# Attention and feed-forward in one program: the last tokens of two heads in one padded tile, and a new table of the order

## The chip, the cores and the metric

The kernel runs on one core of a Trainium2 chip. A core has five engines that run beside each other, each in its own order: TensorE (PE, matmuls; its weight loads are listed as PEld), VectorE (DVE), ScalarE (ACT), GpSimd (POOL) and SyncE (SP, which here only issues DMAs). ACT and POOL issue DMAs too. Matmul results land in PSUM, eight banks of which each tile of results takes one; everything else that is computed on lies in SBUF.

The metric is the device time of one execution in microseconds (us). One execution was also taken with the hardware profiler: "span" is the time from its first to its last instruction, and all start times are from the start of that span.

## What is computed

Attention with exponential features over 8 batches, 8 heads, 576 tokens and 64 dimensions, and then a feed-forward layer on all 4608 tokens:

```
def phi(x):
    proj = np.einsum('bhsd,df->bhsf', x, w_phi)
    proj = proj - np.max(np.abs(proj), axis=-1, keepdims=True)
    return np.concatenate([np.exp(proj), np.exp(-proj)], axis=-1)
q_p, k_p = (phi(q), phi(k))
kv = np.einsum('bhsf,bhsd->bhfd', k_p, v)
z = np.sum(k_p, axis=2)
num = np.einsum('bhsf,bhfd->bhsd', q_p, kv)
den = np.einsum('bhsf,bhf->bhs', q_p, z)[..., None] + 1e-06
...
x = np.ascontiguousarray(attn_out.transpose(0, 2, 1, 3)).reshape(B * S, H * D)
h = np.maximum(np.maximum(x @ w1, x @ w2), x @ w3)
return (h @ w_out).astype(np.float32)
```

`w_phi` is 64x128, `w1` to `w3` are 512x768, `w_out` is 768x512; inputs and output are fp32, the matmuls work in bf16.

## The kernel before

**Units.** Attention is done in 16 units of four heads of one batch, so two units make a batch. The four heads are two pairs (`pr`), each with two heads (`ab`). The 576 tokens of a head are 512 main tokens (`SM`), four tiles of 128, and 64 last ones (`ST`), half a tile.

**The steps of a unit**, by the names that the profile shows: q and k are loaded as bf16 by POOL's DMA queue (`qk_bf`), v as fp32 by SP's (`v_raw`), and the last 64 tokens of q in a load of their own (`tail_raw`), which POOL copies into `qk_bf`. The blocks are transposed into `qkT`, by TensorE in the first four units (`tps`), by DMA transposes from SP's queue in the other twelve. TensorE projects them (`psk`, `psq`, and `pst` for the last tokens); DVE takes the largest absolute value of each row (`mk`, `mq`) and ACT the exponentials of k (`Ek`). For q a second projection gives the features on the partitions (`psm`), and ACT makes `Eq` of it. ACT makes `em` from `mk`, POOL multiplies v by it (`vab`), and TensorE sums `kvps` over the tokens, copied to `kv_sb`. Then come the **numerators**: TensorE multiplies `Eq` by `kv_sb` into two PSUM tiles `psn`, one for each sign of the exponent, with the denominator as 65th column; DVE scales the first by `sq` (L641), adds the second (L644) and inverts the denominators (`rden`, L689); POOL divides (`x_sb`, L690). The result is transposed into `xT`, by TensorE (`pxT`) in the first two units, by a DMA transpose in the others.

**Numerators before.** They are made in four groups, one for each head: five tiles of 65 columns, of which four are its main tokens and the fifth its last ones. The tile of last tokens holds those of both heads of a pair, 64 rows each, and each head of the pair multiplies the whole tile; half of its rows belong to the other head and are not used. So a unit has 20 tiles of numerators, 40 matmuls. `xT` gets ten blocks of 128 columns for each unit. Since the last tokens of the two heads of a pair land in different columns there, `last` copies one half into place on POOL (L896), and then the whole to where the last chunk reads it (L897).

**Feed-forward.** It runs in nine chunks of 512 tokens: the main tokens of each batch, and a last chunk with the last tokens of all batches. A chunk is 12 `ups` groups of four matmuls (L748), relu or maximum on ACT and DVE into `hT`, and four `ops` groups (L781 with four matmuls, L786 with six), which ACT and DVE copy to `osb` for the stores. The first `ups` of a chunk needs `xT` of both units of its batch and the difference of two weight matrices that POOL makes at the start (`w_bf`, L844). TensorE also turns `w1` (`pwT`) and multiplies it by `w_out` (`pm`) before the first `ops`.

**Order.** Every operation is a node, and the string `PLAN` lists all of them by number, with engine, buffer slots and a start time; the program is written out in that order. On each engine instructions run strictly in it, and semaphores make them wait for what they need. Where the table leaves TensorE free in its first 30 us, `fill` puts matmuls of a constant tile there (`idler`, L911), whose results nobody reads.

Of the kernel before, what the change touches and what calls it, by code (L numbers as in the profile page):

```python
# [8 lines left out]
FP32 = mybir.dt.float32  # L9
# [8 lines left out]
DM = H * D  # L18
# [7 lines left out]
HU = 4  # L26
# [6 lines left out]
XW = SM + P  # L33
# [4 lines left out]
BY_HALF = 0  # L38
BY_BATCH = 99
# [10 lines left out]
TRAW = 2  # L50
WD_PE = 0
# [41 lines left out]
115D@11.1 127A@11.8 1166G@11.5 15D@11.7 27T4@12.1 14D@12.0 117A@12.1 120A@12.5 121A@13.0 1167G@12.3 1169G@13.0 130D1@12.2 28D@12.5 43T76@12.8
21T4@13.0 261G@13.8 129D@12.7 46D@13.1 47D@13.5 54A0@13.6 113A@13.8 78T0@13.3 22D@13.8 36T56@14.3 118D@14.1 125D@14.7 56G0@14.0 44A@14.3
114A@14.5 79A@15.0 23T4@14.6 39D@15.3 40A@15.3 24D@15.9 42D@16.3 48T23@16.4 55G@15.1 137A1@15.8 139G1@16.2 80A@16.0 45A@16.2 50D@16.9
116A@16.5 185G@17.3 58A@17.0 108T4@16.7 37A@17.2 334S0@11.6 140G@18.0 263T0@17.2 57A@17.7 59G@18.2 60G@19.3 267T7@17.7 68T13@17.9 61G@20.4
38A@17.8 49D@17.5 81A0@18.3 109D@18.1 264D2@18.7 268D@19.3 41A@18.5 72A@18.9 71A@19.4 138G@20.5 141A@19.9 131T25@18.8 142G@21.6 144A@20.1
62T46@19.1 64A0@20.2 69A@20.3 63A@20.8 70A@21.0 134T07@19.7 132D@19.5 190T3@20.1 65T26@20.6 1168G@22.7 133D@20.1 156T54@21.2 135D@20.7 82T01@21.6
67A@21.4 66A@21.6 161T6@21.9 136D@21.3 158A1@21.7 191D3@21.8 85T27@22.1 159A1@22.2 143G@23.4 83D0@22.4 160A@22.7 86D@22.9 333G0@24.5 157A@23.2
84D@23.3 164A1@23.7 265T3@22.6 163A@23.9 87D@23.7 332G@25.2 162A@24.1 145T04@23.4 146A1@24.4 151T21@23.9 147A@24.5 194T5@24.3 266D@24.1 155A@24.7  # L100
152A@25.2 195D@24.7 1180T7@24.4 93T60@24.8 153A@25.6 88D0@24.9 89G0@26.0 1181D0@25.0 1172G@27.6 90T34@25.1 154A@26.1 94D1@25.6 148T57@25.7 149A@26.6
91D@26.0 283T62@26.3 1178T3@26.5 165T15@27.0 285A0@26.7 284A0@27.0 95D@26.4 92D@26.8 1176T0@27.3 150A@27.3 287D0@27.2 96D1@27.5 1179A@27.4 168T47@27.7
97G@29.7 286D0@27.6 335G@30.9 196T26@28.1 98T3@28.5 166D2@28.0 1177A@28.3 169D@28.4 200A1@29.2 198A1@29.7 176T14@28.9 197A@30.1 167D@28.8 170D@29.2
276T50@29.4 177D0@29.6 99D@30.0 277A@30.6 173T71@30.1 178D@30.4 100T3@31.0 171D2@30.8 202D1@30.9 1170G@31.1 174D@31.5 278A@31.1 281A@31.6 199D@31.9
280A@32.1 175D@32.5 172G1@33.2 1186T4@31.4 1184T7@32.7 192T2@34.0 279D@32.9 210T15@34.6 179D0@33.5 403G1@34.4 337S0@38.0 189S3@39.4 101A@32.5 1187A@33.1
180G@35.1 201A@33.6 203T34@34.7 1185A@34.2 282D@33.6 208A@35.1 1171G@36.3 1173G@38.4 205A@35.6 262S0@40.0 214D1@34.9 269T60@34.9 270A@36.1 274A@36.5
181T7@35.2 1182T5@35.5 1183A@37.0 193D@35.2 183T2@36.8 473S1@40.6 182D@35.8 209D@36.2 204A@37.5 1188T7@37.1 272D@36.8 184D@37.4 213D@37.8 206D@38.1
271A@38.0 1189A@38.6 1194T5@38.4 207A@39.0 301T26@39.3 212A@39.5 275D@38.7 1175G@40.5 294A0@39.8 402G@42.6 1174G@43.3 221A1@40.0 224A0@40.2 305A0@40.3
288T37@39.6 304A0@40.8 303A@41.2 211A@41.7 1195D1@39.4 338S@42.2 336S2@43.9 297A1@42.0 1202T4@39.9 273A@42.1 302A@42.6 404G@45.4 289D@40.0 223G@45.7
612S0@45.8 290D@40.6 1200T5@40.7 1196T3@41.6 222G@47.7 1203D@41.2 291T76@42.6 228T41@42.8 229A1@43.2 1201D@41.8 1197D@42.7 230A1@43.7 218T50@43.0 293D@43.3  # L110
1206T2@43.3 238T3@44.2 1192T6@44.3 220D@43.9 232A@44.2 219D@44.5 406S1@47.4 1207D@45.1 239A@44.6 240A@44.9 1193A@45.4 215T40@45.3 306T53@45.5 292D@45.7
231A@45.8 216D@46.2 217D@46.8 1214T2@45.8 1204T6@46.7 1215D@47.4 310A@46.3 1205D@48.0 307A@46.8 309A@47.3 475S1@50.0 1198T7@47.5 241A0@47.7 339T14@48.5
# [12 lines left out]
541G@69.6 1226A3@71.3 395D@71.2 610G@70.3 386D@71.6 397D@72.0 485T64@71.8 490A1@72.2 545S2@67.5 492T03@72.0 496D1@72.4 750G2@71.0 398D@72.7 399D2@73.3
387D@73.5 489A1@72.7 486A@73.2 680G@71.7 1238T5@72.2 493A@73.7 491D0@73.9 435G@72.4 546S@75.8 1242T2@73.1 1219S@77.0 494A@73.9 478T37@74.1 487A@74.2
1239A0@74.7 495D@74.5 484D@74.8 391D0@75.4 1243A@75.2 481D@75.5 616S0@77.6 1254T1@74.4 450T4@75.3 451A@75.6 1240T0@75.4 751S1@80.4 544S0@82.0 400G1@74.5
482A@75.9 488D@76.1 1255D@76.7 483A@76.4 452A@76.9 1252T5@76.2 440T26@77.2 613G@75.7 479A@77.1 1241D@77.3 437T74@77.4 480A@77.6 441A@78.1 443A@78.6
1253D@78.1 615S@82.6 547T10@78.6 1236T3@78.9 503A1@79.0 442A@79.2 444A@79.7 439D1@78.8 1234T5@79.7 553D1@79.1 438D@79.7 550D@80.0 505G0@79.4 1237A@80.2
465T42@80.6 466D1@81.1 549A0@80.7 506G@81.5 462T76@80.9 463D@81.5 467D@81.9 1250T3@81.2 548A0@81.2 1235A@81.7 454T41@82.1 551A@82.2 504G@81.6 552A@82.6  # L130
1227A@83.1 510T75@82.5 514A1@83.7 1246T2@82.8 455D0@82.6 464D@83.0 456D@83.4 511A1@84.2 1223S@84.0 468D1@83.8 512A@84.7 392G@83.7 1251D@83.9 457T40@83.7
458D@84.5 401S@85.0 1232T6@84.0 1233A@85.1 1248T1@84.9 561T34@85.8 513A@85.6 1247D@84.9 554T72@85.9 459D@85.5 565D0@86.1 563A@86.1 469G2@84.9 584T60@86.2
562A@86.4 821G3@86.1 460D2@86.5 461G@86.8 1249D@86.6 1244T5@86.5 587A0@86.7 470S@88.1 614S2@89.6 564D@87.2 588A0@87.1 1260T4@87.3 559A@87.6 556A@88.1
500T13@88.3 1245D@87.5 497T05@88.5 1261T@88.8 585A@88.6 586A@89.1 560D@88.2 557D@88.8 572A0@89.5 1256T6@90.1 502D@89.4 520T3@91.0 555A@89.7 684S1@90.2
# [121 lines left out]
def kernel(  # L256
# [82 lines left out]


    units = [dict() for _ in range(UNITS)]
    tails, loads, qk_bufs = {}, {}, [None]

    def k_rows(src, u, p0, p1):
        h0 = (u % 2) * HU
# [597 lines left out]
```

## Time and profile before

| | us |
|---|---|
| median of three runs (281.70, 282.66, 283.45) | 282.66 |
| the profiled execution | 282.56 |
| its span | 280.8 |
| what lies around the span | 1.76 |
| TensorE's first `ups` starts at | 40.81 |
| TensorE's last matmul ends at | 276.2 |

A row of a group reads: line, engine, operation, what is written from what is read, shape, count, then busy time, mean duration of one in ns, and the idle time of the engine just before. A row of the timeline reads: start, length, engine, line, operation, count, and in brackets the idle time before it with what ended it. A row of the windows gives for one stretch its length and then for each engine the busy time and the number of instructions. Operations that follow each other overlap a little, so the time from the start of one to the start of the next is less than the duration of one; both are used below, and named.

### The profile page before, as it was taken

How to read it: one execution, taken by the hardware profiler on the slowest of the kernel's cores; microseconds unless marked ns; L12 is line 12 of the kernel's file. 1: busy time of each engine (PE TensorE's matmuls, PEld its weight loads, DVE VectorE, ACT ScalarE, POOL GpSimd, SP SyncE). 2: the span in 40 equal slices, each digit the busy share in tenths (PEclk: the TensorE clock that was granted, in tenths of full speed). 3: DMA queues.
4: the chain of work that ended last, by engine and by line, in shares of the span. 5: the costliest groups of instructions: out<-in, count | busy, mean ns of one | idle time of the engine just before them, and what ended most of it. 6: DMA issues, size and time to landing. Idle time of an engine off the chain costs nothing. (4 is left out here: it accounts for less than half of the span.)

```text
span 280.8 us, 8401 instructions
## 1 busy us (share of the span) xinstructions
PE 268.3 (96%) x3409; PEld 150.8 (54%) x3447; DVE 217.3 (77%) x442; ACT 199.1 (71%) x489; POOL 161.5 (58%) x161
## 2 busy tenths in 40 slices
PE   8789899999999999999999999999999999999993
PEld 5457654576655555555555456655546544444441
DVE  2799989999999969889997899898876871157320
ACT  4799999999999787698978879989589200310001
POOL 4879999998949703897336848393495341000000
PEclk9999999999999999999999999999999999999999
DMA  7999999997999999999999997717130224110253
GB/s 136 300 202 208 207 173 310 260 164 132 171 186 249 236 196 281 169 171 144 189 263 204 188 276 125 151 55 170 39 86 3 77 47 121 40 75 0 82 144 112
DMA packets 76214, 44.52 MB, mean 159 GB/s; under 512 B 52688, under 2 KB 67344, under 8 KB 76176
## 3 DMA queue, kind: packets, MB, share of 16 engines
q1 hardware_dynamic: 59536, 29.21, 49.8%
q0 software_dynamic: 14912, 11.77, 28.7%
q10 hardware_dynamic: 1728, 3.02, 3.0%
q8 instruction: 27, 0.44, 0.7%
q14 instruction: 11, 0.09, 0.1%
HBM read 34.64 MB, written 9.44 MB: 157 GB/s over the span
## 5 line engine op out<-in xcount | busy, mean ns | idle before, releaser
L748 PE MATMUL ups<-xT,w_bf 128*128 128x512 bf16 x414 | 101.3, 379 | 1.0
L584 ACT ACTIVATE Eq<-psm 128x512 bf16<-128x512 f32 (+1 forms) x160 | 81.7, 587 | 5.4 <-PE psm L593 3.1
L548 POOL TENSOR_TENSOR vab<-v_raw,em 128x1152 bf16<-128x1152 f32 (+1 forms) x36 | 68.2, 1907 | 22.9 <-ACT em L542 15.0
L504 ACT ACTIVATE Ek<-psk 128x512 bf16<-128x512 f32 x128 | 72.1, 633 | 8.2 <-PE psk L496 6.3
L748 PEld LDWEIGHTS <-w_bf 128*128 128x128 bf16 x432 | 39.2, 98 | 43.9 <-issue 2.3
L690 POOL TENSOR_TENSOR x_sb<-y,rden 128x640 bf16<-128x640 f32 x32 | 39.9, 1256 | 39.5 <-DVE rden L689 39.0
L786 PE MATMUL ops<-wout_bf,hT 128*128 128x512 bf16 (+2 forms) x214 | 50.5, 373 | 0.3
L758 DVE TENSOR_TENSOR hT<-hT,ups 128x512 bf16<-128x512 bf16 x54 | 35.5, 677 | 13.3 <-PE ups L748 11.1
L500 DVE TENSOR_REDUCE mq<-psq 128x4 f32<-128x512 f32 x64 | 41.2, 682 | 3.5 <-PE psq L496 3.2
L500 DVE TENSOR_REDUCE mk<-psk 128x4 f32<-128x512 f32 x64 | 41.9, 679 | 2.1 <-PE psk L496 1.7
L762 ACT ACTIVATE hT<-ups 128x512 bf16<-128x512 f32 x36 | 21.9, 620 | 24.5 <-PE ups L748 24.4
L641 DVE TENSOR_TENSOR y<-psn,sq 128x325 f32<-128x325 f32 x64 | 30.4, 491 | 6.7 <-PE psn L632 4.3
L796 ACT COPY osb<-ops 128x512 f32<-128x512 f32 x20 | 12.2, 608 | 32.3 <-PE ops L786 31.8
L786 PEld LDWEIGHTS <-hT 128*128 128x128 bf16 x222 | 20.6, 98 | 22.5 <-issue 0.2
L632 PEld LDWEIGHTS <-Eq 128*128 128x128 bf16 x640 | 26.3, 98 | 10.3 <-issue 0.4
L644 DVE TENSOR_TENSOR y<-y,psn 128x325 f32<-128x325 f32 x64 | 29.7, 487 | 1.6
L632 PE MATMUL psn<-kv_sb,Eq 128*128 128x65 bf16 x640 | 28.8, 194 | 0.2
L496 PEld LDWEIGHTS <-qkT 64*128 64x128 bf16 x576 | 18.0, 94 | 13.4 <-issue 8.3
L781 PE MATMUL ops<-xT 128*128 128x512 bf16 x87 | 23.7, 380 | 0.5
L567 PE MATMUL kvps<-vab,Ek 64*128 64x65 bf16 x1152 | 22.1, 191 | 0.8 <-POOL vab L548 0.6
L567 PEld LDWEIGHTS <-Ek 64*128 64x128 bf16 x1152 | 20.3, 94 | 3.4 <-issue 1.3
L796 DVE COPY osb<-ops 128x512 f32<-128x512 f32 (+2 forms) x17 | 11.1, 657 | 12.5 <-PE ops L786 12.5
(65 smaller groups left out, 263.9 us busy)
## 6 DMA issues: line engine op xcount, KB each, us to landing
v_raw<-in_v_dram SPq DMA_DIRECT2D x15, 576.0 KB, 6.0
out_dram<-osb SPq DMA_DIRECT2D x23, 256.0 KB, 3.3
qk_bf<-in_k_dram POOLq DMA_DIRECT2D x15, 288.0 KB, 6.9
qk_bf<-in_q_dram POOLq DMA_DIRECT2D x15, 256.0 KB, 8.7
w_bf<-in_moe_w_dram POOLq DMA_DIRECT2D x3, 768.0 KB, 13.2
out_dram<-osb ACTq DMA_DIRECT2D x9, 256.0 KB, 3.4
tail_raw<-in_q_dram SPq DMA_DIRECT2D x16, 64.0 KB, 4.8
wout_bf<-in_moe_w_out_dram POOLq DMA_DIRECT2D x1, 768.0 KB, 19.2
```

The lines of the kernel that those rows point to most:

```text
L500: return nd(kind, {"DVE": 0.598 if n == 4 else 0.331}, lambda: nc.vector.tensor_reduce(dst(m()), ps()[:, 0:n, :], AXX, ALU.max, apply_abso ...
L504: return nd("ek", {"ACT": 0.478 if n == 4 else 0.264}, lambda: nc.scalar.activation(dst(Ek[g]()), ps()[:, 0:n, :], EXP, scale=1.0 - 2.0 * ...
L548: made.append(chosen(n_, lambda n_, g=g, t0=t0, t1=t1: (nc.vector if n_.eng == "DVE" else nc.gpsimd).tensor_tensor(vab()[:, g, t0:t1, 0:D] ...
L567: nc.tensor.matmul(kvps[ab]()[:, pr, g, :], lhsT=Ek[g]()[r, t, :], rhs=vab()[r, g, t, :], start=(pr == prs[0] and g + j == 0), stop=(pr == ...
L584: return nd("eq", {"ACT": 0.478 if n == 4 else 0.264}, lambda: nc.scalar.activation(Eq[g]()[:, t0:t0 + n, :], ps()[:, 0:n, :], EXP, scale= ...
L632: nc.tensor.matmul(psn[g]()[:, i, :], lhsT=Eq[g]()[:, t, :], rhs=kv()[:, pr, ab, g, :], start=True, stop=True)
L641: n_ = nd("xu", {"DVE": 0.064 + 0.0676 * n_t}, lambda: nc.vector.tensor_tensor(yv(y()), ps(0), sq_of(sq()).unsqueeze(len(shape) - 1).to_br ...
L644: return nd("xw", {"DVE": 0.064 + 0.0674 * n_t}, lambda: nc.vector.tensor_tensor(yv(y()), yv(y()), ps(1), ALU.add), [n_], [psn[1], y], loc ...
L690: divs[pr] = nd("x", {"POOL": 1.2}, lambda pr=pr, y=y, rden=rden: nc.gpsimd.tensor_tensor(x_sb()[:, pr].rearrange("p t a d -> p a t d"), y ...
L748: nc.tensor.matmul(ups()[:, o * n:(o + 1) * n], lhsT=w_bf[i + (not plain)][:, ct, jj * P:(jj + 1) * P], rhs=tokens_of(ct)[:, cols] if halv ...
L758: nc.vector.tensor_tensor(dst, dst, src, ALU.max)
L786: nc.tensor.matmul(ops_()[:, 0:hi - lo], lhsT=hT()[:, j, tt * P:(tt + 1) * P], rhs=wout_bf[:, j, lo:hi], start=plain and j == 0, stop=(j = ...
```

## The change

The last tokens are loaded so that heads 0 and 2 share one tile and heads 1 and 3 the other (one load of two DMAs for each unit instead of one for two units). Their exponentials go into a tile of their own, `eq_ends`, that holds for each sign and each tile three pieces of 64 columns: those of the one head, zeros, those of the other. POOL writes the zeros once at the start. A numerator tile of last tokens is then the sum of two matmuls, one with the columns of the first head and zeros, one with zeros and the columns of the second, each with its own head's `kv_sb`. A unit has 16 + 2 = 18 tiles of numerators, taken in three groups of six; the third holds the last tokens. `sq` is made by one activation instead of two. `xT` gets nine blocks for each unit, and `last` is one copy. Options that were switched off are taken out. The table is new.

```
-XW = SM + P
+XB = PT * P
...
-TRAW = 2
+TRAW = 4
...
 PLAN = """
-9G0@1.2 10S0@0.8 3A@1.1 1D@0.8 2G@1.9 16S0@1.3 0G@2.1 103G1@2.7 104G@7.2 4A@1.8 12D@4.0 8G@7.5 6D@4.2 11A@4.0
...
-    xT = const.tile([P, B, CT, XW], BF16, name="xT")
+    xT = const.tile([P, B, 2, XB], BF16, name="xT")
+    eq_ends = const.tile([P, ES, 2, 2, 3, ST], BF16, name="eq_ends")
...
+    n_zero = node("zero", 0, {"DVE": 0.25, "POOL": 0.45}, None, [], [], port=True)
+    chosen(n_zero, lambda n_: (nc.vector if n_.eng == "DVE" else nc.gpsimd).memset(
+        eq_ends.rearrange("p e g r z c -> p (e g r) z c")[:, :, 1, :], 0.0))
...
-        if u % 2 == 0:
-            t_raw = tails["raw"] = buf("tail_raw", TRAW, [P, 2 * HU // 2, D], FP32)
-
-            def load_t(n_):
-                ends = q[b, :, SM:S, :].rearrange("(pr ab) i d -> ab i pr d", ab=2)
-                for ab in range(2):
-                    queue_of[n_.eng].dma_start(t_raw()[ab * D:(ab + 1) * D, :, :], ends[ab])
...
+        t_raw = buf("tail_raw", TRAW, [P, 2, D], FP32)
+
+        def load_t(n_):
+
+            ends = q[b, h0:h0 + HU, SM:S, :].rearrange("(a r) i d -> a i r d", r=2)
+            for a in range(2):
+                queue_of[n_.eng].dma_start(t_raw()[a * ST:(a + 1) * ST], ends[a])
...
-        eqs["t"] = [q_exp(a, psm, 2, g, NQ) for g in range(2)]
...
+        eqs["t"] = [nd("eq", {"ACT": 0.264}, lambda g=g: nc.scalar.activation(
+            Et()[:, g, :, 0:3:2, :], psm()[:, 0:2, :].rearrange("p r (z c) -> p r z c", z=2), EXP, scale=1.0 - 2.0 * g),
+                       [a, n_tab], [psm, Et], locks=[psm]) for g in range(2)]
...
+        sq = buf("sq", MS, [P, UT], FP32)
+        n_sq = nd("S", {"ACT": 0.1}, lambda: nc.scalar.activation(sq(), mq(), EXP, scale=-2.0), reds_q, [mq, sq])
+        x_sb = buf("x_sb", XSB, [P, UT, D], BF16)
+        divs = []
+        for th in range(3):
+            mine = range(6 * th, 6 * th + 6)
+            ends = th == 2
+            prs = range(2) if ends else sorted({t // 8 for t in mine})
+            psn = [bank("psn", [P, 6, W]) for _ in range(2)]
+
+            def nmm(mine=mine, psn=psn):
+                for i, t in enumerate(mine):
+                    for g in range(2):
+                        o = psn[g]()[:, i, :]
+                        if t < NQ:
+                            pr, c, ab = t // 8, t // 2 % 4, t % 2
+                            nc.tensor.matmul(o, lhsT=Eq[g]()[:, 8 * (c % 2) + 4 * pr + 2 * ab + c // 2, :], rhs=kv()[:, pr, ab, g, :],
                                              start=True, stop=True)
...
+                            continue
+                        for pr in range(2):
+                            pad = Et()[:, g, t - NQ, pr:pr + 2, :].rearrange("p z c -> p (z c)")
+                            nc.tensor.matmul(o, lhsT=pad, rhs=kv()[:, pr, t - NQ, g, :], start=(pr == 0), stop=(pr == 1))
...
+            divs.append(nd("x", {"POOL": 0.767}, lambda th=th, y=y, rden=rden: nc.gpsimd.tensor_tensor(
+                x_sb()[:, 6 * th:6 * th + 6, :], y()[:, :, 0:D], rden().to_broadcast([P, 6, D]), ALU.mult),
+                           [n_], [y, rden, x_sb], port=True))
...
+                nc.sync.dma_start_transpose(out=xT[:, b, u % 2, :].rearrange("p (t c) -> p t c", c=P),
+                                            in_=x_sb().rearrange("p t d -> p (t d)"))
...
-        nc.gpsimd.tensor_copy(xT[D:P, b, :, SM:SM + ST], xT[D:P, b, :, SM + ST:XW])
-        nc.gpsimd.tensor_copy(x_last[b // 4][:, :, b % 4 * ST:(b % 4 + 1) * ST], xT[:, b, :, SM:SM + ST])
+        nc.gpsimd.tensor_copy(x_last[b // 4][:, :, b % 4 * ST:(b % 4 + 1) * ST].rearrange("p (u c) n -> p u c n", u=2),
+                              xT[:, b, :, 2 * SM:XB].rearrange("p u (c n) -> p u c n", n=ST))
```

How the instructions stand before and after, at three places. The first is POOL's queue at the program's start, where it loads q and k of the first units (`qk_bf<-in_q_dram`, `qk_bf<-in_k_dram`) and prepares constants; before:

```order
L383 DMA qk_bf<-in_q_dram 128x2x256
L330 MEMSET wph_low 64x128
masks.py:197 MEMSET ident 128x128
masks.py:199 ISA
masks.py:199 AFFINE_SELECT ident<-ident 128x128
L393 DMA qk_bf<-in_k_dram 128x2x576
L430 CAST qk_bf<-tail_raw 128x2x64
L383 DMA qk_bf<-in_q_dram 128x2x256
```

and now:

```order
L332 MEMSET eq_ends 128x8x64
masks.py:197 MEMSET ident 128x128
masks.py:199 ISA
masks.py:199 AFFINE_SELECT ident<-ident 128x128
L373 DMA qk_bf<-in_q_dram 128x2x256
L330 MEMSET wph_low 64x128
L373 DMA qk_bf<-in_q_dram 128x2x256
L378 DMA qk_bf<-in_k_dram 128x2x576
L408 CAST qk_bf<-tail_raw 128x2x64
L378 DMA qk_bf<-in_k_dram 128x2x576
```

The zeros of `eq_ends` and the identity now stand ahead of the first load of q, and the first copy of last tokens behind three loads instead of two.

The second place is SP's queue at the start, which loads k of the first unit (`k_raw`), the last tokens and v; before:

```order
L408 DMA k_raw<-in_k_dram 128x576
L426 DMA tail_raw<-in_q_dram 64x4x64 x4
L408 DMA k_raw<-in_k_dram 128x576
L435 DMA v_raw<-in_v_dram 128x2x576 x2
L426 DMA tail_raw<-in_q_dram 64x4x64 x2
```

and now:

```order
L387 DMA k_raw<-in_k_dram 128x576 x2
L405 DMA tail_raw<-in_q_dram 64x2x64 x6
L413 DMA v_raw<-in_v_dram 128x2x576
L405 DMA tail_raw<-in_q_dram 64x2x64 x4
L454 DMA_TRANSPOSE qkT<-qk_bf 128x8x128
```

Both halves of k of the first unit now come first, the first v stands behind six DMAs of last tokens, and the second v has left this queue (ACT's queue has it).

The third place is DVE at the end of the second unit's numerators, up to the last copy of `xT` that the first chunk waits for (`mk`, `mq` are row maxima of later units, `pm` is the product of `w1` and `w_out`); before:

```order
L641 TENSOR_TENSOR y_894<-psn_901,sq_677 128x325
L500 TENSOR_REDUCE mk_918<-psk_850 128x4
L644 TENSOR_TENSOR y_894<-y_894,psn_903 128x325
L500 TENSOR_REDUCE mk_834<-psk_884 128x4
L689 RECIPROCAL rden_952<-y_894 128x10
L500 TENSOR_REDUCE mk_834<-psk_886 128x4
L500 TENSOR_REDUCE mq_984<-pst_970 128x2
L472 COPY qkT_602<-tps_956 128x1024
L718 COPY xT_75<-pxT_998 128x640
L500 TENSOR_REDUCE mk_918<-psk_976 128x4
L500 TENSOR_REDUCE mk_834<-psk_986 128x4
L718 COPY xT_75<-pxT_1018 128x640
```

and now:

```order
L614 TENSOR_TENSOR y_940<-psn_881,sq_724 128x390
L478 TENSOR_REDUCE mk_493<-pst_917 128x2
L764 CAST xT_75<-pm_925 128x512
L617 TENSOR_TENSOR y_940<-y_940,psn_883 128x390
L478 TENSOR_REDUCE mk_977<-psk_903 128x4
L619 RECIPROCAL rden_986<-y_940 128x6
L478 TENSOR_REDUCE mk_977<-psk_905 128x4
L635 COPY xT_75<-pxT_960 128x384
L635 COPY xT_75<-pxT_982 128x384
L478 TENSOR_REDUCE mk_977<-psk_951 128x4
L478 TENSOR_REDUCE mk_977<-psk_949 128x4
L635 COPY xT_75<-pxT_1017 128x384
```

A product copy (`xT<-pm`) that was ACT's has come to DVE, the last copy of `qkT` there has gone to ACT, and `xT` is filled by copies of three blocks instead of five.

More of the change, by code (lines that the diff above doesn't have):

```diff
@@ L93 @@
[L93 to L100, printed above, removed]
@@ L341 @@
     units = [dict() for _ in range(UNITS)]
-    tails, loads, qk_bufs = {}, {}, [None]
     def k_rows(src, u, p0, p1):
@@ new lines, in attention, with tx @@
+            for th in range(3):
+                pxT = bank("pxT", [P, 3, P], BF16)
+                def tx(th=th, pxT=pxT):
+                    for o in range(3):
+                        t = 6 * th + 2 * o
+                        nc.tensor.transpose(pxT()[:, o, :], x_sb()[:, t:t + 2, :].rearrange("p a d -> p (a d)"), ident)
+                a = nd("X", {"PE": 0.168}, tx, [divs[th], n_ident], [x_sb, pxT])
+                n_ = nd("Xc", {"DVE": 0.265, "ACT": 0.377}, None, [a], [pxT], locks=[pxT])
+                done.append(chosen(n_, lambda n_, th=th, pxT=pxT: copy_on[n_.eng](
+                    xT[:, b, u % 2, 3 * P * th:3 * P * (th + 1)].rearrange("p (a c) -> p a c", c=P), pxT())))
@@ L726, in attention @@
+            done.append(nd("X", {"SP": 1.21}, xdma, divs, [x_sb], xfer=[(72, 18.0, 1.21)]))
         un["done"] = done
@@ new lines, in chunk, with up, ev @@
+        plain = c_i < RAW0
+        for i in range(2 + plain):
+            for j in range(JT):
+                ups = bank("ups", [P, SM])
+                def up(i=i, j=j, ups=ups):
+                    for ct in range(CT):
+                        nc.tensor.matmul(ups(), lhsT=w_bf[i + (not plain)][:, ct, j * P:(j + 1) * P], rhs=tokens_of(ct),
+                                         start=(ct == 0), stop=(ct == CT - 1))
+                a = ff(("up", "up2", "up3")[i], {"PE": 0.863}, up, ready + ([w_nodes[i]] if plain else diffs[i][j // 2]), [ups])
+                if plain:
+                    plains.append((i, j, a))
+                def ev(n_, i=i, j=j, ups=ups):
+                    dst, src = hT()[:, j, :], ups()
+                    if i > 0:
+                        nc.vector.tensor_tensor(dst, dst, src, ALU.max)
+                    elif plain:
+                        copy_on[n_.eng](dst, src)
+                    elif n_.eng == "ACT":
+                        nc.scalar.activation(dst, src, RELU)
+                    else:
+                        nc.vector.tensor_scalar_max(dst, src, 0.0)
+                e = ff(("t1", "h", "h")[i], {"ACT": 0.477, "DVE": 0.598} if i == 0 else {"DVE": 0.598}, None,
+                       [a] + [before.get(j)] * (i > 0), [ups, hT], locks=[ups])
+                before[j] = chosen(e, ev)
+                if i == 1 + plain:
+                    evac.append(e)
```

460 lines of the change are left out of this document (154 added, 306 removed).

## The prediction

> **What bounds the kernel now.** First the page: the span, the engines' shares, TensorE's busy tenths in 40 slices, and the chain that ended last.
>
> ```profile
> span 280.8 us, 8401 instructions
> PE 268.3 (96%) x3409; PEld 150.8 (54%) x3447; DVE 217.3 (77%) x442; ACT 199.1 (71%) x489; POOL 161.5 (58%) x161
> PE   8789899999999999999999999999999999999993
> PE 44%; POOL 1%; issue 0%; ACT 0%; ACTq 0%
> ```
>
> TensorE is busy all along except at both ends, and the chain consists of TensorE alone but for 1% of POOL. A busy share says little about a stage, so next come the windows: per stretch the length, then busy time of PE, PEld, DVE, ACT and POOL. I cut at the events that matter. The second table holds the `idler` matmuls alone, the third their durations.
>
> ```profile
> 0.00:9.30 9.30, 6.57 (x52) 4.16 (x52) 3.45 (x8) 5.16 (x11) 5.49 (x14) 1.00 0.85 191
> 9.30:33.70 24.40, 22.18 (x427) 15.91 (x428) 22.83 (x53) 22.47 (x66) 21.84 (x27) 1.00 1.23 218
> 33.70:40.80 7.10, 7.00 (x63) 4.07 (x66) 6.20 (x15) 6.79 (x14) 7.08 (x6) 1.00 1.17 177
> 40.80:150.00 109.20, 108.02 (x1544) 60.86 (x1562) 100.30 (x206) 98.17 (x243) 78.68 (x71) 1.00 1.17 208
> 150.00:154.00 4.00, 3.36 (x105) 2.26 (x100) 2.60 (x5) 3.23 (x7) 2.84 (x3) 1.00 1.24 217
> 154.00:276.30 122.30, 121.18 (x1235) 63.55 (x1247) 81.90 (x159) 62.69 (x152) 45.52 (x44) 1.00 0.41 99
> 276.30:280.80 4.50, 0.00 (x0) 0.00 (x0) 0.00 (x0) 0.59 (x1) 0.00 (x0) 1.00 0.42 117
> ```
>
> ```profile
> 0.00:9.30 9.30, 5.16 (x26) 1.00 0.85 191
> 9.30:33.70 24.40, 6.29 (x31) 1.00 1.23 218
> ```
>
> ```profile
> L911 PE MATMUL idler<-idle 128*128 128x256 bf16 x14 | 3.2, 415 | 1.1 <-DVE idle L328 1.1
> L911 PE MATMUL idler<-idle 128*128 128x256 bf16 x7 | 1.0, 282 | 0.0
> ```
>
> Up to 33.7 us TensorE does little that counts: 28.75 busy, of which 11.45 are idlers, so 33.7 - 17.3 = 16.4 us are free or filled. There DVE, ACT and POOL are the bound (22.83, 22.47 and 21.84 of 24.4). From 33.7 to 276.3 TensorE idles 0.10 + 1.18 + 0.64 + 1.12 = 3.04 us; this part is its own work. The last 4.5 us are one copy and the last store. The time is thus the start of the first `ups` (40.8), TensorE's work behind it, its few gaps, and a fixed end.
>
> What releases that first `ups` is seen in the timeline: POOL's last division, TensorE's transposes, DVE's copy.
>
> ```profile
> 36.91 1.27 POOL L690 TENSOR_TENSOR x_sb<-y,rden 128x640 bf16<-128x640 f32 x1
> 39.23 0.44 PE L707 MATMUL pxT<-ident,x_sb 128*128 128x128 bf16 x5
> 39.84 0.48 DVE L718 COPY xT<-pxT 128x640 bf16<-128x640 bf16 x1
> 40.81 1.03 PE L748 MATMUL ups<-xT,w_bf 128*128 128x512 bf16 x4
> ```
>
> **The change part by part.** The groups by line, the shapes apart (columns: busy us, mean ns, idle before):
>
> ```profile
> L632 PE MATMUL psn<-kv_sb,Eq 128*128 128x65 bf16 x640 | 28.8, 194 | 0.2
> L641 DVE TENSOR_TENSOR y<-psn,sq 128x325 f32<-128x325 f32 x64 | 30.4, 491 | 6.7 <-PE psn L632 4.3 <-PE psm L600 1.5 <-ACT Eq L584 0.8
> L689 DVE RECIPROCAL rden<-y 128x10 f32<-128x10 f32 x32 | 6.4, 206 | 0.2
> L690 POOL TENSOR_TENSOR x_sb<-y,rden 128x640 bf16<-128x640 f32 x32 | 39.9, 1256 | 39.5 <-DVE rden L689 39.0 <-PE psn L632 0.4
> L548 POOL TENSOR_TENSOR vab<-v_raw,em 128x576 bf16<-128x576 f32 x8 | 9.1, 1154 | 2.5 <-ACT em L542 2.5
> L548 POOL TENSOR_TENSOR vab<-v_raw,em 128x1152 bf16<-128x1152 f32 x28 | 59.1, 2123 | 20.4 <-ACT em L542 12.5 <-issue 6.4 <-DMA v_raw<-in_v_dram 1.6
> L896 POOL COPY xT<-xT 64x256 bf16<-64x256 bf16 x8 | 3.2, 398 | 4.0 <-DMA xT<-x_sb 3.5
> masks.py:197 POOL MEMSET ident<- 128x128 bf16 x1 | 0.2, 224 | 0.0
> L927 POOL MEMSET const-float32-0.0<- 128x1 f32 x1 | 0.1, 98 | 0.2 <-issue 0.2
> 28.56 0.89 DVE L644 TENSOR_TENSOR y<-y,psn 128x325 f32<-128x325 f32 x2
> tail_raw<-in_q_dram SPq DMA_DIRECT2D x16, 64.0 KB, 4.8
> ```
>
> *TensorE.* Two tiles fewer, but each tile of last tokens now takes two matmuls for each sign: 12 + 12 + 8 + 8 = 40 for a unit, as before (640 in 16 units). Nothing is saved. Two transposes fewer in units 0 and 1 are 2 x 0.055 us (five end in 0.44, one lasts 0.22). So the engine that bounds keeps its work. The second group of six spans both head pairs and needs `kvps` of both, but both stand ahead of the numerators in the old order too, so no wait is added.
>
> *DVE.* Two operations of 325 columns start 0.40 apart (0.89 - 0.49). 390 columns are 20% more; between 0.40 (all fixed) and 0.48 (all by column) I take 0.47, as most of it goes with the columns. A unit: 8 x 0.40 = 3.2 becomes 6 x 0.47 = 2.8, and a third reciprocal costs up to 0.21: 0.2 saved a unit, 3 us in all, hidden behind TensorE but for the two units of the ramp (0.4). [...]
>
> *POOL.* The two shapes of `vab` give 969 ns for 576 columns, 1.68 ns each, and 185 ns fixed. A division of 384 is then 0.83, three are 2.49 against 2 x 1.256 = 2.51: nothing. Eight copies of 398 ns go (3.2 us), late and off the path. The zeros: 224 ns for 128 columns and 98 for one make 1 ns a column, so 0.6 us for 512; by the copies of 256 in 398 ns it could be 0.8. With the identity, which also moves ahead, the first load of q starts about 1.1 us later; it is hidden, since `psk` and four exponentials of k now stand before it is needed, and costs up to 1.1 if they run out.
>
> *DMAs.* 16 more loads of last tokens, 0.68 us of SP's time each (2.72 for four), 11 us in all. SP has room, since it waits longer than this, for `osb` alone 33 us:
>
> ```profile
> 1.19 2.72 SPq L426 DMA_DIRECT2D tail_raw<-in_q_dram  x4
> 4.60 0.94 SPq L435 DMA_DIRECT2D v_raw<-in_v_dram  x2
> SPq L800 <- DVE osb L796: 33.0, 9, 14.6
> PE kvps L567 <- POOL vab L548: 0.6, 1, 0.6
> ```
>
> At the start the first v stands behind two k and six of these: 0.74 + 2 x 0.5 + 6 x 0.68 = 5.8 instead of 4.60, 1.2 us later. `vab` waited for `em` then, not for v (below), which hides it; if v comes last, up to 1.2 are lost on POOL.
>
> Transposes of `xT` shrink from ten blocks to nine, off the path. `sq` by one activation saves ACT one of two short ones a unit, hidden.
>
> *The ramp.* Three waits of POOL and DVE show where it is long:
>
> ```profile
> 3.88 0.33 DVE L415 CAST qk_bf<-k_raw 128x320 bf16<-128x320 f32 x1 [2.88 <-DMA k_raw<-in_k_dram]
> 6.06 0.28 POOL L430 CAST qk_bf<-tail_raw 128x128 bf16<-128x128 f32 x1 [2.52 <-DMA tail_raw<-in_q_dram]
> 15.75 3.38 POOL L548 TENSOR_TENSOR vab<-v_raw,em 128x576 bf16<-128x576 f32 x3 [2.53 <-ACT em L542]
> ```
>
> ```profile
> L858 DVE COPY hT<-pwT 128x1024 bf16<-128x1024 bf16 x1 | 0.7, 692 | 0.0
> L500 DVE TENSOR_REDUCE mk<-psk 128x4 f32<-128x512 f32 x64 | 41.9, 679 | 2.1 <-PE psk L496 1.7
> L472 DVE COPY qkT<-tps 128x1024 bf16<-128x1024 bf16 x3 | 2.0, 682 | 0.0
> ```
>
> Ahead of the last copy of `xT` the new order puts on DVE two copies of `w1` turned, one of the product and two maxima more, and two long copies of `qkT` fewer: three long operations, 0.6 each from start to start (0.68 less the 0.09 by which two `y` overlap), 1.8 us. Three short copies of `kv_sb` more and two short operations fewer are about nothing. With the saving of 0.4 it is 1.5 us more work. On POOL it is 0.6 more (the zeros). Against that stands idle time. DVE is idle 5.85 + 1.57 + 0.90 = 8.3 us up to 40.8; the first 3.8 wait for k and stay, 4.5 can be filled: both halves of k now come first, so casts, reductions and last tokens of unit 0 move into 5 to 10 us. POOL's two waits can shrink by what now stands before them. If all 4.5 go, `ups` starts 3.0 us earlier; if nothing, 1.5 later. I take the middle, 0.7 earlier. Behind it TensorE has a little less left: ahead of the first `ups` now stand eight `psq` and two `psm` more, 0.22 us each set at full rate, less the 0.11 of transposes: 0.3 us. For the gaps I take 0.3 off the 3.04, as DVE and POOL carry 3 us less each; bounds are 3.0 off or 3.0 more. Sum, against the profiled run (282.56 = 280.8 + 1.76, 0.1 below the median): 282.56 - 0.7 - 0.3 - 0.3 = 281.26, so 281.2.
>
> **The rivals.**
>
> *Slower: POOL stands for last tokens.* Every cast now waits for two DMAs of its own unit, and `vab` is queued behind it, then `kvps`. Before, a load served two units, and half of the casts found it there. One stand of 2.52 us is in the ramp above; a late `vab` reached TensorE once (0.6). If in two later units POOL stands 2.5 us and TensorE has nothing else in its order, 5.0 are lost: 282.56 - 1.3 + 5.0 = 286.3. It decides from 1.3 us on. Against it: a load lands in 4.8 us and is issued well ahead. Chance 0.09.
>
> *No change.* The ramp's gaps are refilled by its extra work, and what DVE saves is hidden anyway: 282.3. Chance 0.24, as DVE gets 1.5 us more.
>
> *Slower by the clock.* There are 44 idlers for 57. The trace shows 415 ns for each of the first 14 and 282 for the next 7, so TensorE starts slow and rises after some 3.2 us. If it fell again in the ramp, the 15.9 us of real work in 24.4 make 2.1 in 3.2 us, which would double: 283.3. No gap above 1.6 us is seen before. Chance 0.03. [...]
>
> *Much faster.* The ramp's waits nearly all go (2.2 of 3.0), and a third of the gaps: 282.56 - 2.2 - 0.3 - 1.0 = 279.1. For it: POOL's waits and most of DVE's lie before 16 us, where the orders differ most. Chance 0.16.
>
> **How the numbers follow.** The forecast (280 to 282) has 0.48. Below 1% of a difference (2.8 us) this kernel can't be told from no change, so the limits are 279.8 and 285.5: faster 0.18 (the last rival and a little of the forecast), slower 0.07 (most of the first), same 0.75. The range 278.9 to 284.6 leaves out the first rival and half of the last's spread.
>
> **What would show it.** `psn` again 640 matmuls and about 28.8 us; y at 48 + 48 operations near 0.56 us; the first `ups` between 39 and 41 us; idle time of TensorE from there to its last matmul near 2.7; an end of 4.5. It is wrong if the first `ups` starts after 41.5, if `kvps` waits for `vab` by more than 2 us in sum, or if idlers beyond the first 14 last 400 ns.

## The result and the profile after

The changed kernel takes 290.86 us (median of 4, 289.69 to 292.77) against 282.63 before: a ratio of 1.030, 95% interval 1.023 to 1.036. The profiled execution took 290.7 us, of which 288.7 are its span. In e4_x4_early, e5_small_dma, e6_shift and e10_shift_only single executions (two of four, two of ten, three of ten, one of four) took over 1.5% longer than the fastest one; the medians below include them, the ratios leave them out.

First the page of the changed kernel: the span, TensorE's busy time, its tenths in 40 slices, the granted clock in tenths, and the chain that ended last.

```profile
span 288.7 us, 8420 instructions
PE 272.4 (94%) x3432; PEld 150.8 (52%) x3432; DVE 210.6 (73%) x428; ACT 199.2 (69%) x472; POOL 157.3 (54%) x171
PE   8879999999997949999999999999998999999993
PEclk9999999999999996999999999999999999999999
PE 72%; DMA 12%; POOL 7%; ACT 3%; issue 2%; SPq 1%; DVE 1%; POOLq 0%; DVEq 0%; ACTq 0%
```

Two digits of TensorE's row are new, the 7 and the 4, and right behind the 4 the clock has a 6. The chain, TensorE alone before, now runs 12% through DMAs. TensorE's waits name what it stood for (total, times, longest):

```profile
PE ups L660 <- DMA xT<-x_sb: 4.2, 1, 4.2
PE psn L603 <- issue: 1.8, 1, 1.8
PE kvps L546 <- issue: 1.2, 1, 1.2
PE kvps L546 <- POOL vab L527: 0.3, 1, 0.3
```

The timeline gives their places, and the first `ups`; the windows, cut at these places, show TensorE's busy time first and the granted clock behind POOL's.

```profile
39.82 2.76 PE L660 MATMUL ups<-xT,w_bf 128*128 128x512 bf16 x12
88.13 0.22 PE L603 MATMUL psn<-kv_sb,Eq 128*128 128x65 bf16 x2 [1.81 <-issue]
108.67 4.42 PE L660 MATMUL ups<-xT,w_bf 128*128 128x512 bf16 x10 [4.20 <-DMA xT<-x_sb]
213.66 2.43 PE L546 MATMUL kvps<-vab,Ek 64*128 64x65 bf16 x141
```

```profile
85.80:88.10 2.30, 0.52 (x11) 0.39 (x10) 1.14 (x3) 2.07 (x6) 1.72 (x1) 1.00 1.69 277
104.50:108.70 4.20, 0.03 (x1) 0.02 (x1) 1.19 (x4) 2.37 (x6) 1.53 (x2) 0.81 1.28 180
108.70:113.90 5.20, 5.20 (x22) 1.86 (x23) 1.76 (x3) 0.76 (x2) 0.00 (x0) 0.50 1.15 297
215.90:217.40 1.50, 0.25 (x17) 0.13 (x11) 0.19 (x1) 0.12 (x1) 0.00 (x0) 1.00 0.00 0
284.40:288.70 4.30, 0.00 (x0) 0.00 (x0) 0.00 (x0) 0.57 (x1) 0.00 (x0) 0.92 0.38 108
```

So the span's 7.9 us more can be accounted for. The first `ups` starts at 39.8 for 40.8: -1.0. TensorE stands 4.2 for `xT` at 104.5. Behind that the clock is 0.50 for 5.2 us (ten `ups` matmuls take 4.42 us there, twelve took 2.76 at 39.82), and half of it is lost: 2.6. Two stands in the middle of a row of matmuls, put on nothing ("issue"), are 1.8 and 1.25. Less for `vab` (0.6 to 0.3) and a shorter end (4.5 to 4.3) give -0.5. Sum 8.35; the 0.45 over is smaller gaps and work, not taken apart.

Why `xT` was late is on SP's queue and in the DMA issues. First SP's timeline, of before and of the changed kernel, where it transposes `xT` of units 4 and 5:

```profile
90.38 4.11 SPq L722 DMA_TRANSPOSE xT<-x_sb  x2
```

```profile
85.59 1.44 SPq L413 DMA_DIRECT2D v_raw<-in_v_dram  x1
87.20 6.83 SPq L454 DMA_TRANSPOSE qkT<-qk_bf  x2
94.08 0.57 SPq L413 DMA_DIRECT2D v_raw<-in_v_dram  x1
94.69 1.28 SPq L405 DMA_DIRECT2D tail_raw<-in_q_dram  x2
96.08 5.25 SPq L639 DMA_TRANSPOSE xT<-x_sb  x2
102.12 2.73 SPq L413 DMA_DIRECT2D v_raw<-in_v_dram  x2
```

Then the issues from 76 to 104 us (count, KB each, median us to landing), of before and of the changed kernel:

```profile
v_raw<-in_v_dram SPq DMA_DIRECT2D x2, 576.0 KB, 5.4
xT<-x_sb SPq DMA_TRANSPOSE x2, 4.2
```

```profile
v_raw<-in_v_dram SPq DMA_DIRECT2D x5, 576.0 KB, 8.8
xT<-x_sb SPq DMA_TRANSPOSE x2, 8.8
```

Five loads of v stand where two stood, and `xT` lands in 8.8 us for 4.2. Over the whole run the 14 transposes of `xT` land in these times, first before, then now:

```profile
DMA to landing us min/median/max: 3.3/3.6/7.2
DMA to landing us min/median/max: 3.2/3.5/10.8
```

The longest, 10.8, is the one that TensorE stands for: unit 5's goes out at 97.9 and lands at 108.6. Before, it went out at 93.1 and landed 3.5 us later. So 4.8 us of its lateness are SP's, which comes to it later, and 7.3 the transfer's. The table tells which are new ahead of `xT`: the loads at 85.6 and 94.1 are v of units 11 and 10, which it sends out at 80.5 and 87.2 of its own time, though their first uses stand at 142 and 135. Theory A: these bytes (or the issues) make `xT` late. Theory B: SP holds `xT` behind transposes of `qkT` that wait for other engines.

### The profile page after: what moved, and what is told of

It is laid out like the page before. It is cut to its first block, busy times and chain, and to the rows that moved or that the text cites. A ratio compares the mean times of both kernels' runs of the same rounds, so it can differ in the third digit from the quotient of the medians.

```text
span 288.7 us, 8420 instructions
## 1 busy us (share of the span) xinstructions
PE 272.4 (94%) x3432; PEld 150.8 (52%) x3432; DVE 210.6 (73%) x428; ACT 199.2 (69%) x472; POOL 157.3 (54%) x171
## 4 chain that ended last, share of the span: by engine, by line
PE 72%; DMA 12%; POOL 7%; ACT 3%; issue 2%; SPq 1%; DVE 1%; POOLq 0%; DVEq 0%; ACTq 0%
PE ups L660 30%; PE ops L697 14%; PE ops L692 10%; PE kvps L546 5%; PE psn L603 5%; DMA xT<-x_sb 4%; DMA v_raw<-in_v_dram 3%; POOL vab L527 3%; DMA qkT<-qk_bf 3%; PE psk L474 2%; PE psm L572 2%; DMA tail_raw<-in_q_dram 2%; PE psq L474 2%; ACT Ek L482 2%; PE psn L608 1%
## 5 line engine op out<-in xcount | busy, mean ns | idle before, releaser
L660 PE MATMUL ups<-xT,w_bf 128*128 128x512 bf16 x432 | 104.0, 385 | 4.2 <-DMA xT<-x_sb 4.2
L482 ACT ACTIVATE Ek<-psk 128x512 bf16<-128x512 f32 x128 | 73.9, 640 | 6.3 <-PE psk L474 4.0
L563 ACT ACTIVATE Eq<-psm 128x512 bf16<-128x512 f32 x128 | 71.7, 630 | 7.5 <-PE psm L572 6.2
L620 POOL TENSOR_TENSOR x_sb<-y,rden 128x384 bf16<-128x384 f32 x48 | 38.9, 824 | 38.9 <-DVE rden L619 28.6
L673 ACT ACTIVATE hT<-ups 128x512 bf16<-128x512 f32 x40 | 24.9, 634 | 23.6 <-PE ups L660 21.9
L614 DVE TENSOR_TENSOR y<-psn,sq 128x390 f32<-128x390 f32 x48 | 26.3, 556 | 4.4 <-PE psn L603 2.2
L617 DVE TENSOR_TENSOR y<-y,psn 128x390 f32<-128x390 f32 x48 | 26.3, 556 | 2.4 <-DVE y L614 0.5
L603 PEld LDWEIGHTS <-Eq 128*128 128x128 bf16 x512 | 21.9, 98 | 10.4 <-issue 3.1
L603 PE MATMUL psn<-kv_sb,Eq 128*128 128x65 bf16 x512 | 24.1, 194 | 1.9 <-issue 1.8
L675 DVE TENSOR_SCALAR hT<-ups 128x512 bf16<-128x512 f32 x14 | 9.3, 685 | 20.7 <-PE ups L660 20.7
```

The source lines that it names most:

```text
L482: return nd("ek", {"ACT": 0.478 if n == 4 else 0.264}, lambda: nc.scalar.activation(dst(Ek[g]()), ps()[:, 0:n, :], EXP, scale=1.0 - 2.0 * ...
L563: return nd("eq", {"ACT": 0.478 if n == 4 else 0.264}, lambda: nc.scalar.activation(Eq[g]()[:, t0:t0 + n, :], ps()[:, 0:n, :], EXP, scale= ...
L603: nc.tensor.matmul(o, lhsT=Eq[g]()[:, 8 * (c % 2) + 4 * pr + 2 * ab + c // 2, :], rhs=kv()[:, pr, ab, g, :], start=True, stop=True)
L620: divs.append(nd("x", {"POOL": 0.767}, lambda th=th, y=y, rden=rden: nc.gpsimd.tensor_tensor(x_sb()[:, 6 * th:6 * th + 6, :], y()[:, :, 0: ...
L660: nc.tensor.matmul(ups(), lhsT=w_bf[i + (not plain)][:, ct, j * P:(j + 1) * P], rhs=tokens_of(ct), start=(ct == 0), stop=(ct == CT - 1))
```

## The experiments

Each is the changed kernel with the edit shown, unless said otherwise.

**The v loads of units 11 and 10 later** (e1_v_late). The two words of the table:

```diff
-822S2@80.5    753S0@87.2
+822S2@127.5   753S0@118.3
```

> The changed kernel with two numbers of its table altered: the v of units 11 and 10 is loaded by SP after 127.5 and 118.3 in the table's time instead of 80.5 and 87.2 (first used at 142 and 135), so both 576 KB loads leave the stretch ahead of the xT transposes of units 4 and 5. Theory A (these early v loads crowd the DMA engines and SP, so xT lands 4.2 us late and TensorE then runs 6.8 us at half rate, 2.6 lost): the wait of ups for xT at 104 falls below 1 us, the clock stays at 1.00, and the time is 290.9 - 6.8 = 284 (283 to 285.5). Theory B (xT is late because SP holds it behind qkT transposes that wait for POOL and TensorE): both stay, 289 to 291.

285.09 us, ratio to before 1.010 (1.005 to 1.015), span 281.9. In the issues of the same stretch three v loads are left, `xT` lands in 6.3, TensorE waits for it nowhere, and the clock is 1.00 throughout. What is left of TensorE's waits is the two stands without a name:

```profile
v_raw<-in_v_dram SPq DMA_DIRECT2D x3, 576.0 KB, 7.4
xT<-x_sb SPq DMA_TRANSPOSE x2, 6.3
```

```profile
PE psn L603 <- issue: 1.8, 1, 1.8
PE kvps L546 <- issue: 1.2, 1, 1.2
```

The span falls by 6.8, which is 4.2 + 2.6 (the medians fall by 5.8; the profiled execution is the fastest of its four). Theory A holds for this wait; theory B, by which it would have stayed, falls.

**The unit 4 transpose earlier** (e4_x4_early).

```diff
-403S@89.4
+403S@80.4
```

> The changed kernel with the xT transpose of unit 4 at 80.4 in the table instead of 89.4, ahead of a v load, two qkT transposes, another v load and tail loads on SP; unit 5's stays. Theory B (xT held behind the others on SP): the two transposes no longer run one behind the other, unit 5's lands 2 to 4 us sooner, the wait falls to 0.5 to 2 us with no half rate: 284 to 287. Theory A (traffic, and unit 5 is last anyway): the wait stays within 1 us, 290 to 291.5.

291.02 us, ratio 1.020 (1.011 to 1.030). In the profiled execution (291.99) `ups` waits 6.0 us, not less. But the four executions lie far apart (286.0 to 292.6), and one of 286.0 would suit theory B. This run does not decide between the two.

**The two loads issued by ACT** (e3_v_act).

```diff
-822S2@80.5    753S0@87.2
+822A2@80.5    753A0@87.2
```

> The changed kernel with the v loads of units 11 and 10 at the same place of the table, but issued by ACT instead of SP. The bytes stay, SP's issue time (0.8 to 1.4 us each) goes. If the bytes are what delays xT (theory A, traffic): the wait stays at 3 to 4.5 us and the time at 289.5 to 291.5. If it is SP's time (theory A, queue): the wait falls by 1.5 to 2.5 us and the half-rate stretch with it, 284.5 to 287.

291.62 us, ratio 1.032 (1.027 to 1.036), but for another reason: ACT stood before it could issue the first load, and TensorE waited 6.7 us for ACT.

```profile
89.81 0.39 ACTq L413 DMA_DIRECT2D v_raw<-in_v_dram  x1
90.24 0.60 ACT L482 ACTIVATE Ek<-psk 128x512 bf16<-128x512 f32 x1 [7.17 <-DMA out_dram<-osb]
```

The run does not tell bytes from issues; its time only happens to match one theory. The next was made for it.

**Small loads in their place** (e5_small_dma): e1_v_late, and at 80.5 and 87.2 SP loads 32 KB instead.

```diff
+    small = const.tile([P, 2, D], FP32, name="small")
+    for i, at in enumerate((80.5, 87.2)):
+        order.append(Node("small", 0, {"SP": 0.42}, lambda i=i: nc.sync.dma_start(small[:, i, :], v[0, i, 0:P, :]), [], []))
...
```

> The kernel of the late v loads (285.1 us), with a small load (128x64, 32 KB) from SP at each of the two places where the 576 KB loads stood. SP issues as many DMAs as in the changed kernel, the bytes are gone. If the bytes made xT late: as without them, no wait of ups over 1 us, 284 to 286. If it was SP's time for the two issues: the wait of 2 to 4 us and the half rate return, 288 to 291.

285.17 us, ratio 1.009 (1.005 to 1.013), and in the profile no wait for `xT`. As many issues of SP as in the changed kernel cost nothing here; what is left is the bytes.

**The same fault put into the kernel before** (e7_before_v_early): v of units 13 and 9 ahead of `xT` of units 4 and 5.

```diff
-961S3@99.6   683S1@108.2
+961S3@82.3   683S1@84.5
```

> The kernel before, with the v of units 13 and 9 loaded at 82.3 and 84.5 in its table instead of 99.6 and 108.2, ahead of the xT transposes of units 4 and 5: nothing else is changed. If early v loads alone make xT late: ups waits 1 to 5 us for xT near 101 us, with a half-rate stretch if it is over 2.6, and the time goes from 281.9 to 284 to 289. If the tile arrangement or the rest of the new order is needed for it: no wait, 281 to 283.5.

285.66 us, ratio 1.010 (1.007 to 1.014). The size came, the place did not: `xT` was in time (its two transposes landed in 6.5 us for 4.2, in the middle), and TensorE stood at 88 for ACT, whose store of an output went out at 88.12, by the chain of waits behind a load of last tokens.

```profile
83.69 4.35 DMA tail_raw<-in_q_dram
88.06 0.02 ACTq L800
88.12 0.35 ACTq L800
88.52 1.57 ACT Eq L584 x3
```

The windows there show the wait (1.9 us by TensorE's waits) and, from 90.8 on, half the clock, 0.50:

```profile
88.10:90.10 2.00, 0.17 (x4) 0.05 (x1) 1.17 (x4) 1.58 (x4) 1.84 (x3) 1.00 0.95 331
90.80:94.20 3.40, 3.40 (x10) 1.02 (x8) 1.60 (x3) 3.40 (x9) 0.00 (x0) 0.50 1.18 138
```

So two early v loads cost 1% with the old tiles and the old order too. How they did is not shown: the load of last tokens took 4.35 us, no longer than such loads do in this stretch of the kernel before (4.5), so it was not their bytes that made it late, and what held the store stays open.

**The wait filled with idlers.** In the first trial (e2_fill) 36 idlers stand ahead of the `ups` that waits; in the second (e8_fill) they are one node with one tile.

```diff
+    for n in order:
+        if n.num == 1281:
+            b = next(b for b in n.bufs if b.pool is banks)
+            todo += [(n.start - 0.01, make(b.index))] * 36
```

> The changed kernel with 36 idler matmuls (128x256, 0.11 us each, 4.0 in all) put on TensorE right ahead of the first ups of the chunk that waits for xT. They fill the wait and delay nothing if xT lands when it did. If the half rate behind the wait is due to the idle time: the granted clock is 1.00 throughout, and 2.6 us come back, 288.3 (287.3 to 289). If the half rate has another cause (the table's dense stretch, power): it shows up again and the time stays at 290.9 or a little over.

298.15 us, ratio 1.056 (1.051 to 1.060): worse, since my filler was bad. Each idler had a tile of its own in one bank and seems to have waited for the one before (10.2 us idle ahead of 35 of them); 17 ran in the first 3.6 us, and then the clock fell all the same, for 13.7 us. The filler held TensorE until 116.8, though `xT` had landed at 110.9.

```profile
102.50:106.10 3.60, 2.99 (x17) 1.07 (x14) 1.83 (x5) 3.00 (x8) 2.07 (x3) 1.00 1.10 100
106.10:119.80 13.70, 12.27 (x33) 3.69 (x33) 0.00 (x0) 0.00 (x0) 0.00 (x0) 0.50 1.24 235
```

```diff
-            todo += [(n.start - 0.01, make(b.index))] * 36
+            todo.append((n.start - 0.01, make(b.index, 36)))
...
-    def product(i):
+    def product(i, times=1):
...
+            for _ in range(times):
```

> The changed kernel with 36 idlers ahead of the waiting ups, all into one bank and with no wait between them (in the earlier trial each waited for the one before and TensorE was half busy). 4 us of dense work in place of the idle 4.2: if the clock falls for lack of work, it stays at 1.00 and the time is 290.9 - 2.6 = 288.3 (287 to 289.5). If not, the half rate is seen again and the time is 290 to 293.

287.52 us, ratio 1.015 (1.011 to 1.019). The clock stays at 1.00 through the same stretch, and 3.3 us come back. That is 0.7 more than the 2.6 expected; the second stand without a name (1.25) is gone too in its profile, with 72 instructions more ahead of it, and the first is 1.1 for 1.8.

```profile
102.40:106.60 4.20, 4.20 (x58) 3.58 (x57) 3.08 (x8) 4.14 (x10) 2.65 (x4) 1.00 1.28 112
```

**88 instructions more** (e6_shift): e1_v_late, with each idler of the ramp in two halves. What led there: the two stands lie 3,584 = 14 x 256 instructions of TensorE apart, counted through the trace (3,577 matmuls and weight loads, 7 semaphore instructions), and the page has a DMA queue for programs, whose 27 packets of 16 KB stand for 6,864 matmuls and weight loads, about 254 each. One packet arrives at the very place of the second stand (the issues from 214.9 to 216.1 us hold nothing else):

```profile
q8 instruction: 27, 0.44, 0.6%
```

```profile
q8 instruction: 1, 0.02, 4.6%
```

From these two counts I took 256 instructions for a packet, an estimate.

```diff
-            nc.tensor.matmul(idler[:, 0:2 * P], lhsT=idle, rhs=idle.unsqueeze(1).to_broadcast([P, 2, P]), start=True, stop=True)
+            for half in range(2):
+                nc.tensor.matmul(idler[:, half * P:(half + 1) * P], lhsT=idle, rhs=idle, start=True, stop=True)
```

> The kernel of the late v loads, with each of the 44 idlers of the ramp split in two matmuls of 128 columns: the same busy time, 88 more instructions of TensorE ahead of everything from 30 us on. Theory F (the two stands that the profile puts on nothing, 1.78 and 1.25 us in the middle of a row of matmuls, are waits for the next 16 KB of TensorE's program, which arrive by DMA): both stand 256 x 14 instructions apart, so the place where they can occur moves by 88 instructions; the second goes (there 256 instructions last 2.0 us, at the moved places 4.8 at least), the first goes or shrinks, span 281.9 - 1.3 to -3.0 = 279 to 280.6, time 281.5 to 284. Rival (the waits belong to those matmuls, by data or a bank): both stay at the same matmuls, 284 to 286.5.

282.04 us, ratio to before 0.995 (0.992 to 0.998). Both stands are gone, and nothing but the ramp was touched; the same matmuls run through. The span falls by 1.6, not by the 3.05 of the two stands, since a wait for `xT` shows again: TensorE comes to the old place at 102.8 for 104.5, and `xT` of unit 5 lands at 104.2 for 102.3:

```profile
PE ups L660 <- DMA xT<-x_sb: 1.5, 1, 1.5
```

**The split idlers alone** (e10_shift_only), the v loads early as in the changed kernel.

> The changed kernel with split idlers alone; the v loads are early as in it. By the account (waits 4.2 for xT, 2.6 of half rate, 1.8 and 1.25 for program code): the 1.8 ahead of the xT wait is only handed on to it, the 1.25 behind it is saved, so 290.9 - 1.25 = 289.6 (288.5 to 291); the xT wait grows to 4 to 6.5 us. If the two code waits add up with the rest: 287.9 or less.

288.44 us, ratio 1.020 (1.014 to 1.025): 2.4 less than the changed kernel (2.9 by the two ratios), closer to the whole 3.05 than to the 1.25 I had expected. The wait for `xT` is 4.4, about as long as in the changed kernel, so the stand ahead of it was not merely handed on: `xT` of unit 5 too landed sooner, at 107.3 for 108.6.

**A version that beats both** (e9_mended): late v loads, split idlers, and

```diff
-403S@89.4   820S0@87.8
+403S@80.4   820S0@91.5
```

> The changed kernel with late v loads and split idlers as in the run of 282.0 us, and two more moves in its table: the xT transpose of unit 4 at 80.4 instead of 89.4 and the last tokens of unit 11 loaded at 91.5 instead of 87.8, both so that unit 5's xT leaves SP sooner. If the xT wait that is left there (1.5 us) is all that stands between this order and its own work: the wait goes, span about 279, time 280.3 to 281.5, ratio to before 0.992 to 0.998, and no run near 290. If the transposes are held up by the bytes of q, k and stores alone: the wait stays over 1 us and the time at 281 to 283.

280.66 us against 282.32 of before on the same chip: ratio 0.993 (0.990 to 0.996), all twelve executions between 280.4 and 281.7. The profiled one (281.73) is the slowest, and its windows show what may be the reason: there is no wait after the first `ups`, but the clock fell in the ramp, and the first `ups` starts at 41.4 for 40.3 in e6_shift, which has the same ramp.

```profile
19.40:26.20 6.80, 6.56 (x103) 5.04 (x97) 6.12 (x12) 5.90 (x16) 6.77 (x10) 0.50 1.20 209
41.40:100.00 58.60, 58.38 (x884) 32.95 (x883) 53.69 (x108) 52.53 (x132) 49.73 (x47) 1.00 1.17 204
100.00:110.00 10.00, 10.00 (x175) 5.89 (x174) 9.19 (x21) 9.51 (x24) 6.21 (x8) 1.00 1.22 262
```

This doesn't show that the new tiles alone are worth 0.7%: the kernel before was not given moves of its own.

## Why the prediction was wrong

*What the edit itself costs* was right. The groups of the changed kernel (busy us, mean ns):

```profile
L603 PE MATMUL psn<-kv_sb,Eq 128*128 128x65 bf16 x512 | 24.1, 194 | 1.9 <-issue 1.8
L608 PE MATMUL psn<-kv_sb,eq_ends 128*128 128x65 bf16 x128 | 6.5, 193 | 0.0
L617 DVE TENSOR_TENSOR y<-y,psn 128x390 f32<-128x390 f32 x48 | 26.3, 556 | 2.4 <-DVE y L614 0.5
```

`psn` is 512 + 128 = 640 again at the same 194 ns (27.9 us together, for 28.8), `y` 48 operations of 556 ns in each half. The divisions, put at 0.83, take 0.824 (38.9 in 48). The ramp, put at -0.7, gave -1.0. The end is 4.3 for 4.5. That most of a `y` goes with the columns was my estimate, shown by no row of the kernel before; in the changed one two of 390 columns in a row take 1.03 us (at 60.59) and one 0.56, so they start 0.47 apart, as taken.

*The gaps* are the step that failed: "For the gaps I take 0.3 off the 3.04, as DVE and POOL carry 3 us less each; bounds are 3.0 off or 3.0 more." By the waits they grew by 4.2 + 1.8 + 1.25 - 0.3, about 7 us, and the half clock behind one of them cost 2.6 beside, for which the sum had no term. DVE and POOL were not late; a transfer was, and the rest was no engine's work at all. The 3.04 was itself read too trustingly: that page has 3,409 matmuls for 3,447 weight loads, the new one 3,432 for 3,432, and a matmul without a record reads as idle time. Of the 41 gaps over 0.02 us that TensorE has in the old trace from its first `ups` on, 37 last 0.05 us each, 2.0 in sum; without them the 2.9 that are idle there are 0.9. In the new trace it is 7.5, where the forecast was 2.7.

*The DMAs* hold the omission behind it. I priced 16 more issues of last tokens on SP and found them hidden; e5_small_dma shows that two further issues of SP cost nothing (285.17 us for 285.09 of e1_v_late). But the order of SP's queue had more in it than these: it moved two v loads of 576 KB by some 50 us to ahead of `xT`. I followed the loads only at the start, where the first v is, and took "a load lands in 4.8 us" from the median of one kind as the cost of every one. In the crowded stretch the loads of v land in 8.8 us for 5.4, the transposes of `xT` in 8.8 for 4.2.

*Slower: POOL stands for last tokens* had the right sign by luck, and the wrong engine. `kvps` waited 0.3 us for `vab`, under the 2 us from which the rival was to be believed.

*Slower by the clock* had the right mechanism at the wrong place. It asked whether fewer idlers let the clock fall in the ramp; in the profiled execution it fell in a wait of 4.2 us, where no idlers stand: 0.81 over the wait, 0.50 behind it. e8_fill shows that it fell by this wait, since with dense work in its place the clock stays at 1.00. In e7_before_v_early it fell behind a wait of 1.9 us. The ramp is not safe either: in the trace of e4_x4_early, whose ramp is the changed kernel's, the clock is at half for 3.4 us from 19.6 on, in e9_mended for 6.8, and their first `ups` start at 40.8 and 41.4, those of the other traces of the new order at 39.8 to 40.3. But the rival should have asked which wait anywhere could reach some microseconds, not about the ramp alone.

*What would show it*: of the five signs four came (640, 0.56, a first `ups` at 39.8, an end of 4.3), the idle time did not (7.5 for 2.7), and none of the three alarms went off. They all watched engines; not one watched the landing of `xT`.

*No change* and *much faster* fell with the gaps. That the order could do 280.7 once its transfers are mended lies near the 281.2 of the forecast, but that is a result of the moves, and no credit to the sum.

## What to carry to other kernels

When a change brings a new order, list for every queue which transfers moved, by how much and with how many bytes, and set against each other the time of issue and of first use: a load that goes out 50 us early can be paid by whatever is needed at that time (here by `xT`, 8.8 us to landing for 4.2). An account of waits needs one line for transfers, one for the clock behind each wait, and one for the stands that no row explains. An engine that bounds the kernel and stands in the middle of a row of like instructions is worth counting instructions for.

## What the hardware did that I had not expected

TensorE waited for its own program: with 88 instructions more ahead of them both stands are gone (e6_shift). Counted in blocks of 256, which is the estimate above, the second stand comes behind a block that is nearly all `kvps` and lasts 2.0 us, where the next shortest block of the changed kernel behind its ramp lasts 4.45; the packet for the next block started 1.2 us after the block began, took 0.88, and TensorE went on 1.4 us after it had landed. The same holds wherever it stood so: in the ten stands of this kind in the traces of the changed kernel, e1_v_late, e3_v_act, e4_x4_early, e5_small_dma and e8_fill it went on 1.2 to 1.6 us after the packet had landed. Why the packet at 85.7 was late is open; the DMA engines had much to do then (share 1.69 in the window above, 1.14 in the 46 us before it), and in e2_fill, with the same program up to there, it started at 84.3 and came nearly in time.

The clock fell on pauses shorter than the 2.6 us from which I had expected it to, and not always. A wait of 1.9 us was followed by 3.4 us at half rate (e7_before_v_early); in one of 4.2 (the changed kernel) it fell after 2.6, for 6.8 us of which 5.2 held work; a filler of 17 idlers in 3.6 us was followed by 13.7 (e2_fill); the wait of 1.5 in e6_shift by none. In the ramp TensorE's longest wait between 12 us and the fall is 0.9 us, at 18.3; the clock fell behind it in two of the ten traces of the new order, e4_x4_early and e9_mended. These half-rate stretches, 3.4 in e4_x4_early and e7_before_v_early, 6.8 in the changed kernel and e9_mended, 13.7 in e2_fill, are near one, two and four times 3.4.

In e3_v_act ACT is idle for 7.2 us around a load that it issues, and all that ACT had queued stood with it; TensorE waited 6.7 us. The profile puts this on the landing of a store; whether that is the reason was not tried.
